# Where and in what shape one weight matrix is loaded in a decode layer: four DMAs early, or 65 spread over the run

## The chip, the cores and the metric

The kernel runs on one core of a Trainium2 chip. The metric is the device time of one execution in microseconds. Before the change it was 1316.74 us, the median of three runs (1316.66 to 1317.19). One more execution was taken by the hardware profiler; all rows shown come from it.

## The reference

One transformer layer decodes one token for each of 4 sequences: layer norm, attention of 32 heads over a cache of 8192 positions, output projection and residual, layer norm, gated feed-forward block, residual. All inputs are bfloat16.

```
B, Sq, D = 4, 1, 512;  H, Sk, Dh = 32, 8192, 128;  F = 1792

q = (layernorm(x) @ wq).reshape(B, Sq, H, Dh).transpose(0, 2, 1, 3)
scores = einsum("bhqd,bhkd->bhqk", q, k_cache) * Dh ** -0.5
p = softmax(scores)
o = einsum("bhqk,bhkd->bhqd", p, v_cache)
h = x + o.transpose(0, 2, 1, 3).reshape(B, Sq, H * Dh) @ wo
n = layernorm(h)
out = h + einsum("bsf,fd->bsd", sigmoid(n @ w_gate) * (n @ w_up), w_down)
```

The two caches hold 4 x 32 heads of 8192 x 128 values each: 128 heads of K and 128 of V, 2 MB apiece, 537 MB together. Each byte is used once. wq and wo have 4 MB each, the three feed-forward matrices 1.8 MB each.

## The kernel before

**Tiling.** A "head" below is one pair of sequence and head, numbered 0 to 127. K's or V's head is one slot of the tile KV, which has eight slots: 128 partitions, 16 KB on each (64 rows of the cache in a row). The PE engine transposes K in blocks of 128 x 128 (L360); ACT and DVE in turn copy the results out of PSUM (L370, L372); PE multiplies them with q (L385). Eight heads make a group, and the 16 groups go through the softmax one after the other. V's head is used nine heads later (LAGH = 9), as it lies in its slot (L469; L481 in the last group). When a group's 8 heads are done, the group's result is brought into the tile OT (L521), and `project` (L490 to L504) multiplies it with the two of wo's 32 head blocks that belong to this group (L498) and adds it to the residual. Group g needs the head blocks 2g and 2g + 1.

**Weights.** wq and wo use the same memory, the tile Wreg (128 partitions of 32 KB), one after the other: wo may be asked for only when the q projection (L533) has read wq. wo lies in HBM as 32 blocks of 128 rows of 512 values, so its view in Wreg takes from each partition's 32 KB one run of 1 KB for each head block.

**Loads and their order.** All DMAs are issued by the SP engine, in one queue and in the order of the list `order` (L305 to L315). Heads of K and V alternate from K's head 9 on (K 9, V 0, K 10, V 1, ...). Into this list are put wq behind K's head 0, wo's four pieces behind K's heads 2, 3, 4 and 5 (L312), w_gate before V's head 125, w_up and w_down at the end. A K or V is issued by `emit_head` (L271): it takes the next of the eight slots in rotation and waits until the job that held the slot has been read. `pump` (L324) takes from the list whatever can be put in the program at that point. A head is one DMA of 2 MB with one run of 16 KB per partition (L277); K's head 0 and V's head 127 come in four pieces (L274).

`emit_wo` (L300) issues one piece: one DMA of 1 MB, 128 partitions with eight runs of 1 KB each, and its token goes into the list t_wo. Each piece has a semaphore of its own (wo0 to wo3), and every DMA adds 16 to its semaphore when it has landed. `project` waits for all four tokens, `*t_wo` (L501).

**The end.** After V's head 127 come the last projection, the second layer norm, the gate and up products (L593), the down product in two halves (L609) and the output's DMA (L619).

Of the kernel before, what the change touches and what calls it, by code (L numbers as in the profile page):

```python
# [13 lines left out]
NKT = 16  # L14
LAGH = 9
GH = 8


class _Prog:
# [27 lines left out]
    def emit(self, eng, fn, waits=(), incs=1):  # L47

        todo = self._waits(eng, waits)
        tok = self.token(eng, incs) if incs else None  # L50

        def run(e):
            for key, v in todo:
                e.wait_ge(self.sems[key], v)
            made = fn(e)
            made = made if isinstance(made, list) else [made]
            if incs:
                assert len(made) == incs
                for m in made:
                    m.then_inc(self.sems[eng], 1)  # L60

        self.ops[eng].append(run)
        return tok
# [14 lines left out]
def bass_sequential_preLN__mha_block_cached__glu_gated_glu__decode_kernel(  # L78
# [20 lines left out]
    NH = B * H  # L99
    NG = NH // GH  # L100
    SCALE = float(DH) ** -0.5
# [3 lines left out]
    prog = _Prog()  # L105
    emit = prog.emit

    with ExitStack() as es:
        def SB(name, shape, dt):
            return es.enter_context(nc.sbuf_tensor(name, shape, dt))  # L110

        ident = SB("ident", [128, 128], BF16)
        identf = SB("identf", [128, 128], FP32)
        M8 = SB("M8", [128, GH], FP32)
        Gmat = SB("Gmat", [128, 128], FP32)
# [10 lines left out]
        q_all = SB("q_all", [128, NH], BF16)  # L126
        Lq = SB("Lq", [128, 2, GH * W], BF16)
        KV = SB("KV", [128, NSL, R * 128], BF16)
        kTc = SB("kTc", [128, NKT, 512], BF16)
        S_sb = SB("S_sb", [128, 512], FP32)  # L130
        E_sb = SB("E_sb", [128, 512], BF16)
        PT = SB("PT", [128, 2, NK * GH * 32], BF16)
        mpart = SB("mpart", [128, 1], FP32)
        mrow = SB("mrow", [1, GH], FP32)
        negmb = SB("negmb", [128, 1], FP32)
        sig = SB("sig", [128, 1], FP32)
        rsum = SB("rsum", [128, 1], FP32)
        O_sb = SB("O_sb", [128, 512], FP32)
        OT = SB("OT", [128, 2, GH], BF16)
        sg_sb = SB("sg_sb", [128, NFT * B], FP32)  # L140
# [7 lines left out]
        wo_v = Wreg[:, :].rearrange("p (h f) -> p h f", h=H)  # L148
# [39 lines left out]
        def cols(t, c):  # L188
            return t[:, c:c + NDC * (B - 1) + 1:NDC]
# [107 lines left out]
        t_wo = []  # L297
        t_qproj = []

        def emit_wo(i):  # L300
            src = A_wo.rearrange("(h p) f -> p h f", p=128)
            t_wo.append(prog.dma("sp", f"wo{i}", lambda e: e.dma_start(  # L302
                wo_v[:, 8 * i:8 * (i + 1), :], src[:, 8 * i:8 * (i + 1), :]), [t_qproj[0]]))

        order = []  # L305
        for n in range(NH):
# [2 lines left out]
        order.sort()  # L309
        order = [(k, n) for _, _, k, n in order]  # L310
        order.insert(1, ("wq", 0))
        for i, after in enumerate((2, 3, 4, 5)):  # L312
            order.insert(order.index(("k", after)) + 1, ("wo", i))
        order.insert(order.index(("v", NH - 3)), ("wg", 0))
        order += [("wu", 0), ("wd", 0)]  # L315
# [8 lines left out]
        def pump():  # L324
            while next_dma[0] < len(order) and ready(*order[next_dma[0]]):
                kind, n = order[next_dma[0]]
                next_dma[0] += 1
                if kind == "k":
                    emit_head("k", n, k_src(n), t_k, "k0p" if n == 0 else "")
                elif kind == "v":  # L330
                    emit_head("v", n, v_src(n), t_v, "vl" if n == NH - 1 else "")
                elif kind == "wq":
                    emit_wq()
                elif kind == "wo":
                    emit_wo(n)
                else:
                    emit_weight(kind)
# [152 lines left out]
        def project(g, t_ot):  # L490
            ob = g % 2

            def f(e):
                ins = None
                for c in range(NDC):
                    for hh in range(2):
                        h = 2 * g + hh
                        ins = e.matmul(cols(bank[XO][:, 64:64 + NDC * B], c), wo_v[:, h, 128 * c:128 * (c + 1)],  # L498
                                       OT[:, ob, B * hh:B * (hh + 1)], start=(hh == 0), stop=(hh == 1))
                return ins  # L500
            t = emit("pe", f, [t_ot, *t_wo])  # L501
            st_["ot"][ob] = t
            st_["h"] = st_["xo"] = emit("dve", lambda e: e.tensor_tensor(
                sth[:, 0:NDC * B], sth[:, 0:NDC * B], bank[XO][:, 64:64 + NDC * B], ALU.add), [t, st_["h"]])  # L504

        def finish(g):
            ob = g % 2
            t_oev[g] = emit("act", lambda e: e.activation(O_sb[:, :], bank[OBK], ACT.Copy),  # L508
                            [t_pvg[g], st_.get("sel")])
            box = {}  # L510

            def s1():
                def f(e):
                    ins = None
                    for q in range(4):
                        ins = e.matmul(bank[XO][:, 0:GH], O_sb[:, 128 * q:128 * (q + 1)],  # L516
                                       selq[:, q:q + 29:4], start=(q == 0), stop=(q == 3))
                    return ins
                t = emit("pe", f, [t_oev[g], t_sel, st_["xo"]])
                st_["sel"] = t  # L520
                box["ot"] = emit("dve", lambda e: e.tensor_copy(OT[:, ob, :], bank[XO][:, 0:GH]),  # L521
                                 [t, st_["ot"][ob]])

            def s2():
                project(g, box["ot"])
            return [(4, s1), (6, s2)]
# [22 lines left out]
        for u in range(4 * (NH + LAGH)):  # L549
# [20 lines left out]
            if vu >= 0:  # L570
                pv(vu // 4, vu % 4)
                if vu % 32 == 31 and vu // 32 < NG - 1:
# [8 lines left out]
        t_ot = emit("dve", lambda e: e.tensor_copy(OT[:, gl % 2, :], bank[OBK][:, 0:GH]),  # L581
                    [t_pvg[gl], st_["ot"][gl % 2]])
        project(gl, t_ot)
        t_hn, _ = layernorm(sth, st_["h"], 1, hnT, bank[XS], st_["xs"])

# [91 lines left out]
```

## Time and profile before

| What | Value |
|---|---|
| median of the runs | 1316.74 us |
| profiled execution, its own time | 1317.24 us |
| its span in the profile | 1315.5 us |
| HBM read | 550.77 MB, 419 GB/s over the span |
| K heads, 127 whole ones | 2048 KB each, 28.7 us from issue to landing (median) |
| V heads, 127 whole ones | 2048 KB each, 33.1 us |
| wo, 4 pieces | 1024 KB each, 14.1 us; issued at 21.4, 25.7, 32.1 and 41.5 us |
| wq, 4 pieces | 1024 KB each, 11.7 us |
| SP at L302 (wo's first piece), wait for the q projection | 15.0 us |
| first projection (L498) | 159.7 us |
| last projection (L498) | 1303.3 us |

The span is the time from the first to the last instruction that the profiler saw; the execution's own time is 1.74 us longer. The part 2 of the page cuts the span into 40 slices and gives the busy tenths of each engine; part 3 gives the DMA queues (q1 carries what the program asks for, q8 and q14 fetch instructions); part 4 follows the work that ended last back to the start and adds up its time by engine. "Issue to landing" is the time from SP's instruction to the last completion step of its DMA, with the time in the queue behind earlier DMAs in it.

### The profile page before, as it was taken

The page shows a single profiled execution, that of the slowest core. Times are in us where ns is not written, and L with a number is a line of the kernel's source. Part 1 is how long each engine was busy: PE and PEld are TensorE (multiplying, and loading weights), DVE is VectorE, ACT ScalarE, POOL GpSimd, SP SyncE. Part 2 cuts the span into 40 slices and gives each one's busy share as a digit, 9 for nine tenths or more (in the row PEclk, how much of TensorE's full clock was granted, in tenths as well). Part 3 has the DMA queues.
Part 4 walks back from the last instruction along what each step waited for, and adds up shares of the span by engine and source line. Part 5 has one row for each costly group of instructions (what it writes and reads, how often), then busy time and mean ns, then how long its engine had stood idle before and what let it go on. Part 6 is the DMA issues. An engine that isn't in the chain of part 4 may idle for free.

```text
span 1315.5 us, 29564 instructions
## 1 busy us (share of the span) xinstructions
PE 1016.4 (77%) x13385; PEld 671.9 (51%) x13385; DVE 721.1 (55%) x1210; ACT 608.7 (46%) x1095; POOL 9.0 (1%) x11
## 2 busy tenths in 40 slices
PE   6887877877788787887788778788887878778764
PEld 5654544545455454554455445455554545545443
DVE  5774655556555565555556456555555656556520
ACT  3664544545444454444445445454444545445420
POOL 2000000000000000000000000000000000000000
PEclk8988888888888888788888888888788888888865
DMA  9999999999999999999999999999999999999996
GB/s 381 415 427 426 427 427 427 425 428 425 428 425 426 427 425 428 424 427 426 427 426 426 426 428 424 427 425 428 427 424 426 426 428 425 426 427 428 425 411 245
DMA packets 45510, 552.68 MB, mean 420 GB/s; under 512 B 4420, under 2 KB 10312, under 8 KB 12360
## 3 DMA queue, kind: packets, MB, share of 16 engines
q1 hardware_dynamic: 45384, 550.79, 99.0%
q8 instruction: 105, 1.72, 0.5%
q14 instruction: 21, 0.17, 0.0%
HBM read 550.77 MB, written 0.00 MB: 419 GB/s over the span
## 4 chain that ended last, share of the span: by engine, by line
DMA 81%; PE 16%; SPq 2%; ACT 0%; issue 0%; DVE 0%
DMA KV<-in_A_v_cache_dram 76%; PE PS L360 10%; PE PS L385 3%; PE PS L469 3%; DMA KV<-in_B_w_down_dram 2%; DMA KV<-in_A_k_cache_dram 1%; SPq L277 1%; DMA Wreg<-in_A_wq_dram 1%; SPq L302 0%; SPq L295 0%; ACT kTc L370 0%; SPq L274 0%; ACT L422 0%; PE PS L533 0%; PE PS L481 0%
## 5 line engine op out<-in xcount | busy, mean ns | idle before, releaser
L372 DVE CAST kTc<-PS 128x512 bf16<-128x512 f32 x1024 | 676.1, 692 | 484.4 <-PE PS L360 481.6
L370 ACT ACTIVATE kTc<-PS 128x512 bf16<-128x512 f32 x1024 | 573.4, 595 | 648.2 <-PE PS L360 646.2
L360 PEld LDWEIGHTS PS<-ident,KV 128*128 128x128 bf16 x8192 | 547.5, 109 | 252.3 <-ACT kTc L370 135.7
L360 PE MATMUL PS<-ident,KV 128*128 128x128 bf16 x8192 | 654.7, 240 | 12.8 <-DMA KV<-in_A_k_cache_dram 10.4
L469 PE MATMUL PS<-KV,PT 128*32 128x512 bf16 x1920 | 216.8, 442 | 242.2 <-DMA KV<-in_A_v_cache_dram 242.2
L385 PE MATMUL PS<-kTc,Lq 128*32 128x512 bf16 x2048 | 227.1, 435 | 1.1 <-DVE Lq L545 0.6
L469 PEld LDWEIGHTS PS<-KV,PT 128*32 128x32 bf16 x1920 | 52.4, 99 | 273.9 <-DMA KV<-in_A_v_cache_dram 273.6
L385 PEld LDWEIGHTS PS<-kTc,Lq 128*32 128x32 bf16 x2048 | 53.5, 95 | 64.6 <-issue 19.1
L481 PE MATMUL PS<-PT,KV 128*128 128x1 bf16 x512 | 14.9, 165 | 18.0 <-DMA KV<-in_A_v_cache_dram 15.4
L481 PEld LDWEIGHTS PS<-PT,KV 128*128 128x128 bf16 x512 | 14.3, 104 | 18.6 <-DMA KV<-in_A_v_cache_dram 15.9
L516 PE MATMUL PS<-selq,O_sb 128*128 128x8 f32 x120 | 16.7, 266 | 7.1 <-ACT O_sb L508 7.1
L516 PEld LDWEIGHTS PS<-selq,O_sb 128*128 128x128 f32 x120 | 15.3, 200 | 10.0 <-ACT O_sb L508 10.0
L409 DVE TENSOR_REDUCE mrow<-PS 1x8 f32<-1x128 f32 x16 | 4.5, 279 | 29.2 <-PE PS L405 29.2
L205 ACT ACTIVATE lnw<-lnw 128x4 f32<-128x4 f32 x2 | 0.4, 205 | 38.9 <-DVE lnw L202 38.9
L581 DVE CAST OT<-PS 128x8 bf16<-128x8 f32 x1 | 0.2, 167 | 32.6 <-PE PS L481 32.6
L521 DVE CAST OT<-PS 128x8 bf16<-128x8 f32 x15 | 2.5, 167 | 19.5 <-PE PS L516 19.5
L422 ACT ACTIVATE E_sb<-S_sb,negmb 128x512 bf16<-128x512 f32 x16 | 11.6, 722 | 3.1 <-DVE negmb L420 2.6
L400 DVE TENSOR_REDUCE mpart<-S_sb 128x1 f32<-128x512 f32 x16 | 11.0, 686 | 3.1 <-ACT S_sb L398 1.5
L508 ACT ACTIVATE O_sb<-PS 128x512 f32<-128x512 f32 x15 | 9.0, 597 | 6.3 <-PE PS L469 6.3
L446 DVE CAST PT<-PS 128x512 bf16<-128x512 f32 x16 | 10.9, 682 | 0.7 <-PE PS L438 0.7
L398 ACT ACTIVATE S_sb<-PS 128x512 f32<-128x512 f32 x16 | 9.6, 597 | 1.2 <-PE PS L385 1.1
L405 PE MATMUL PS<-identf,mpart 128*1 128x128 f32 x32 | 7.5, 325 | 2.4 <-DVE mpart L400 2.4
(67 smaller groups left out, 119.5 us busy)
## 6 DMA issues: line engine op xcount, KB each, us to landing
KV<-in_A_k_cache_dram SPq DMA_DIRECT2D x127, 2048.0 KB, 28.7
KV<-in_A_v_cache_dram SPq DMA_DIRECT2D x127, 2048.0 KB, 33.1
Wreg<-in_A_wq_dram SPq DMA_DIRECT2D x4, 1024.0 KB, 11.7
Wreg<-in_A_wo_dram SPq DMA_DIRECT2D x4, 1024.0 KB, 14.1
KV<-in_A_k_cache_dram SPq DMA_DIRECT2D x4, 512.0 KB, 5.7
KV<-in_A_v_cache_dram SPq DMA_DIRECT2D x4, 512.0 KB, 26.6
KV<-in_B_w_gate_dram SPq DMA_DIRECT2D x1, 1792.0 KB, 28.1
KV<-in_B_w_up_dram SPq DMA_DIRECT2D x1, 1792.0 KB, 26.4
```

Of the source, the lines that this page charges most:

```text
L277: done[n] = [prog.dma("sp", f"sl{slot}", lambda e: e.dma_start(KV[:, slot, :], src), w)] * 4
L360: ins = e.matmul(bankT[g % NTB][:, 128 * i:128 * (i + 1)], KV[:, slot, r * 128:(r + 1) * 128], ident[:, :], start=True, stop=True)
L370: t_copy[g] = emit("act", lambda e: e.activation(kTc[:, ks, :], bankT[g % NTB][:, :], ACT.Copy), w)
L372: t_copy[g] = emit("dve", lambda e: e.tensor_copy(kTc[:, ks, :], bankT[g % NTB][:, :]), w)
L385: mms.append(e.matmul(PS[32 * j:32 * (j + 1), 512 * SBK:512 * (SBK + 1)], Lq[:, g % 2, off:off + 32], kTc[:, (n * NK + k) % NKT, :], start ...
L398: t_sev[g] = emit("act", lambda e: e.activation(S_sb[:, :], bank[SBK], ACT.Copy), [t_score[32 * g + 31], st_.get("exp")])
L400: t_mx = emit("dve", lambda e: e.tensor_reduce(mpart[:, :], S_sb[:, :], AX.X, ALU.max), [t_sev[g], st_.get("p1")])
L422: box["a2"] = emit("act", lambda e: e.activation(E_sb[:, :], S_sb[:, :], ACT.Exp, bias=negmb[:, 0:1], scale=SCALE, accum_out=sig[:, 0:1]), ...
L446: st_["xs"] = t_ptc[g] = emit("dve", lambda e: e.tensor_copy(dst, src), [t, t_pt0, t_pvg.get(g - 2)])
L469: mms.append(e.matmul(PS[32 * j:32 * (j + 1), 512 * OBK:512 * (OBK + 1)], PT[:, pb, o:o + 32], KV[:, slot, 512 * k:512 * (k + 1)], start=f ...
L481: ins = e.matmul(bank[OBK][:, i:i + 1], KV[:, slot, 128 * r:128 * (r + 1)], PT[:, pb, o:o + 1], start=(r == 0), stop=(r == R - 1))
L516: ins = e.matmul(bank[XO][:, 0:GH], O_sb[:, 128 * q:128 * (q + 1)], selq[:, q:q + 29:4], start=(q == 0), stop=(q == 3))
```

## The change

Three things are changed, all of them about wo.

The pieces stand elsewhere in the order: behind K's heads 9, 30, 62 and 94 in place of 2, 3, 4 and 5. They still wait for the q projection.

The pieces are cut otherwise. Pieces 0, 1 and 2 (eight head blocks each) and the first half of piece 3 (four) are loaded by 16 DMAs each, and each of these takes eight partitions that are 4 apart: 32a + j, 32a + j + 4, ..., 32a + j + 28 for a and j from 0 to 3. The second half of piece 3 is one DMA of 128 partitions. This makes 65 DMAs: 48 of 64 KB, 16 of 32 KB and one of 512 KB. All DMAs of a piece add to the piece's semaphore, and the token of the last stands for the piece.

A projection waits for the one piece that holds its head blocks, t_wo[g // 4], and no longer for all four.

```diff
+WO_PIECES = (((0, 8, 8),), ((8, 16, 8),), ((16, 24, 8),), ((24, 28, 8), (28, 32, 16)))
+WO_AFTER = (9, 30, 62, 94)
...
         def emit_wo(i):
+
             src = A_wo.rearrange("(h p) f -> p h f", p=128)
-            t_wo.append(prog.dma("sp", f"wo{i}", lambda e: e.dma_start(
-                wo_v[:, 8 * i:8 * (i + 1), :], src[:, 8 * i:8 * (i + 1), :]), [t_qproj[0]]))
+            for lo, hi, k in WO_PIECES[i]:
+                if k == 16:
+                    parts = [slice(0, 128)]
+                else:
+                    parts = [slice(32 * a + j, 32 * a + j + 29, 4) for a in range(4) for j in range(4)]
+                for ps in parts:
+                    t = prog.dma("sp", f"wo{i}", lambda e, ps=ps, lo=lo, hi=hi: e.dma_start(
+                        wo_v[ps, lo:hi, :], src[ps, lo:hi, :]), [t_qproj[0]])
+            t_wo.append(t)
...
-        for i, after in enumerate((2, 3, 4, 5)):
+        for i, after in enumerate(WO_AFTER):
             order.insert(order.index(("k", after)) + 1, ("wo", i))
...
-            t = emit("pe", f, [t_ot, *t_wo])
+            t = emit("pe", f, [t_ot, t_wo[g // 4]])
```

## The prediction

> **What bounds the kernel now.** I read the page first: the slices of part 2, the queues of part 3 and the chain of part 4.
>
> ```profile
> span 1315.5 us, 29564 instructions
> PE 1016.4 (77%) x13385; PEld 671.9 (51%) x13385; DVE 721.1 (55%) x1210; ACT 608.7 (46%) x1095; POOL 9.0 (1%) x11
> DMA  9999999999999999999999999999999999999996
> q1 hardware_dynamic: 45384, 550.79, 99.0%
> q8 instruction: 105, 1.72, 0.5%
> DMA 81%; PE 16%; SPq 2%; ACT 0%; issue 0%; DVE 0%
> ```
>
> No compute engine is above 77%, the sixteen DMA engines are busy in every slice but the last, and the chain is 81% DMA. The kernel is its 552 MB stream, so what matters is where the sixteen are *not* all busy. Stretches from the view by windows (last two columns: mean busy share of the sixteen, GB/s):
>
> ```profile
> 1100.00:1200.00 100.00, 82.62 (x1060) 54.10 (x1056) 59.19 (x102) 50.75 (x92) 0.00 (x0) 0.86 1.01 426
> 1280.00:1300.00 20.00, 6.32 (x218) 6.08 (x219) 0.00 (x0) 0.00 (x0) 0.00 (x0) 0.50 0.81 317
> 1300.00:1312.00 12.00, 6.61 (x198) 6.02 (x196) 1.84 (x11) 1.71 (x3) 0.00 (x0) 0.50 0.59 212
> ```
>
> Against 1.01, the last 32 us miss 20 x 0.20 + 12 x 0.42 = 9.0 us per engine. From 1292 to 1302 us the share is 0.53: about half the engines work and half are done. Why shows in the completion events. A K or V DMA makes sixteen completion steps, one per engine. For V's head 123 (issued at 1249.2 us) they come 0, 0.1, 0.3, 0.4, 0.8, 2.0, 5.9 and 9.5 us after the first, and then 18.6, 19.0 ... 20.2 us; for V's last whole head the eighth stands at 10.4 and the last at 20.8. Early on all sixteen lie within 1.2 us. Each of q8's 105 instruction fetches throws one engine back by 1.55 us (between two DMAs one of the sixteen steps moves from 9.09 to 10.66), in rotation over eight engines: 105 / 8 x 1.55 = 20.3 us, which is the lag. The other eight (I call them the leading ones) never carry q8, but one of them is thrown back 1.0 us at each of nine fetches on the small instruction queue (q14) and ends at 10.4. Which eight are which the trace does not say by number; where two packets of the two groups start in the same nanosecond, the leading one's record stands first in 23 of 25 cases, so the groups look like a lower and an upper half of one order.
>
> **What is removed and moved.** Before, each of four output-weight DMAs takes all sixteen engines for 2.67 us (first completions 28.05 to 30.71, 35.60 to 38.27, 43.17 to 45.88, 50.77 to 53.43 us): 64 rows of 1 KB per engine, 41.8 ns each, 10.7 us in all. Removing them from the first 60 us saves nothing by itself, since the bytes are asked for later. SP's wait for the q projection, 15.0 us at L302, goes: K's heads 3 to 7 are asked for at about 6 us. It is worth nothing, since the queue held work through it (share 1.03 in 10 to 20 us). The projections wait for one piece instead of four. The first runs at 159.7 us and every fourth after that needs a new piece, some 318 us apart (159.7, 477, 795, 1113); the pieces stand behind K's heads that landed at 75, 284, 602 and 920 us. So 80 to 190 us of slack covers them; the wait costs nothing, and were the cover gone it would be what a piece is late.
>
> **What is added: 64 DMAs of eight rows.** Pieces 0 to 2 are 16 DMAs each of 8 x 8 rows of 1 KB, piece 3 is 16 of 8 x 4 and one of the old form with 4 heads, 65 in place of 4. That a DMA of few rows takes few engines shows in x's load: four rows, four data packets, four completion steps. Eight rows then sit on at most eight engines, and by the order above I take the leading eight. For each of these: 3 x 128 + 64 rows x 41.8 ns = 18.7 us, 1.3 for the last four heads, 64 completion packets of 9 ns for 4, 0.5: 20.6 us against 10.7, **+9.9**. For the fetch eight: 1.3 against 10.7, **-9.4**. Then the last fetch engine ends at 20.8 - 9.4 = 11.4 of the old scale and the six undisturbed leading ones at 9.9 to 11.9: balanced. But the leading engine that already lagged ends at 10.4 + 9.9 = 20.3, against 20.8 before. Every K and V waits for all sixteen, so of 9 us possible **-0.5** remains.
>
> [...] The row of this trace is K's first head in four 512 KB pieces: first completions at 4.55, 5.84, 7.21, 8.47 us, 1.3 apart for 8 rows of 159 ns; fixed parts overlap, and I take none.
>
> **SP and the rings.** SP issues 61 more DMAs at 0.33 to 0.43 us, 20 to 26 us in all, beside 1114 us in which L277 waits: free. Not free is that the queue holds a limited number of rows. SP's own timeline:
>
> ```profile
> 21.42 0.38 SPq L302 DMA_DIRECT2D Wreg<-in_A_wo_dram  x1
> 21.84 3.83 SPq L277 DMA_DIRECT2D KV<-in_A_k_cache_dram  x1
> ...
> 34.66 6.82 SPq L277 DMA_DIRECT2D KV<-in_A_k_cache_dram  x1
> 41.53 0.44 SPq L302 DMA_DIRECT2D Wreg<-in_A_wo_dram  x1
> 42.01 9.40 SPq L277 DMA_DIRECT2D KV<-in_A_k_cache_dram  x4
> ```
>
> A K behind a piece of 65 descriptors per engine (64 rows, one step) held SP for 3.8 to 7.8 us, where 0.33 to 0.43 is usual; after 49.8 us, with the last old piece still queued, it took in more until 9 + 65 + 7 x 9 = 137 were outstanding per engine, so I put the limit near 140. A new piece is 16 x 9 = 144 on the leading engines, on top of some six K and V of 9 each. I expect SP to stick in the middle of a piece until the slowest leading engine has drained its K and V, some 30 us; the next K is queued behind. The fetch eight, with no rows of the piece, then run dry and start again together with the rest. Each piece so wipes out the lags, and the fetch engines' spared 9.4 us are spent idle. Two costs follow. After the last piece (near 925 us) the fetch engines lag anew: 29 fetches / 8 x 1.55 = 5.6 us against 3 x 1.0 for the slow leading one, less 0.3 of head start: **+2.3**. And at each restart the leading engine itself may wait. The bound below is nothing (SP issues in about the 0.34 us that eight rows of 41.8 ns take), above 4 x 2.2 = 8.8 us (an empty queue, as at the start: issue at 1.15, first completion at 4.6 us, less 1.25 of data). I take 0.35 each, **+1.4**, nearer the lower end since small DMAs stay queued while SP goes on.
>
> Where two engines write the same partitions no row tells: half of the small DMAs go to partitions 64 to 127, which the other eight also fill. The bounds are 0 and half speed for that half, 3.5 x 2.67 = 9.4 us; I take 0, since by the paragraph above the other eight are mostly idle then.
>
> **Sum.** -0.5 + 2.3 + 1.4 = +3.2 us. The profiled execution took 1317.24 us (span 1315.5 and 1.74 around it), so it would be 1320.4; the median of the runs is 0.5 lower, so **1319.9 us**. A change under 0.2% (2.6 us) I count as none.
>
> **Rivals.** *Balance:* the slow leading engine's delays are absorbed in the restarts or it gets fewer rows, and all engines end near 11.9 of the old scale: 20.8 - 11.9 = 8.9 us less, 1307.8 at best, 1312 if half of it comes. For it: the 9.0 idle us above, and that 9.4 fits a lag of 8 to 10 between the means of the halves. Against: the sixteen steps, where one leading engine stands at half the lag. *Nothing shifts to the end:* SP does not stick, or the rows spread over all engines; -0.5 to 0, 1316.2 to 1316.7. For it: six K and V were taken in within 3 us behind the fourth old piece. *Overload (slower):* the rows land on engines that carry q8, or meet the other eight's writes at full price. One fetch engine among the eight is enough: 20.8 + 9.9 = 30.7 against 20.8, +9.9, **1326.6**; it decides as soon as a q8 engine ends later than the slow leading one. For it: no row shows which engines eight rows take. Against: the order of equal stamps. [...]
>
> **Chances.** Forecast 0.42, of which 0.27 is above 2.6 us and 0.15 within; balance 0.20; nothing shifts 0.17; overload 0.21. So faster 0.20, same 0.32, slower 0.48. The forecast's own range is 1316.2 (no sticking) to 1327.3 (restarts at 8.8). As both signs hold much of the chance the range reaches to half of the balance and to the overload with a little over: 1311.5 to 1327.5.
>
> **What would show it.** In the changed profile, the eight-row DMAs make eight completion steps or sixteen. The last sixteen steps of V's head 123 within 6 us mean that the lags were wiped out; one step alone near 20, that nothing stuck; eight near 30, overload. A V or K behind a piece holds SP for tens of us, or not. The windows after 1280 us show whether the share stays near 1 to the end: if so, balance has come and my slow leading engine was wrong. If SP's small issues take far more than 0.43 us each without the ring being full, the free 61 DMAs were wrong.

## The result and the profile after

The changed kernel took 1329.08 us (median; 1328.34 to 1330.92) beside 1316.66 us of the kernel before on the same chip: 12.4 us more, ratio 1.0094, 95% interval 1.0083 to 1.0106. The forecast was 1319.9, its range ended at 1327.5. The span grew from 1315.5 to 1326.6 us.

The page of the kernel after: span, engine and DMA slices, queues, and the chain.

```profile
span 1326.6 us, 29627 instructions
DMA  9999999999999999998999999999999999999997
GB/s 384 398 411 425 426 427 427 426 370 425 427 426 427 426 426 427 428 422 366 426 426 427 426 428 425 427 427 395 426 426 426 428 428 425 427 427 427 425 424 277
q1 hardware_dynamic: 45848, 550.79, 98.4%
q8 instruction: 105, 1.72, 0.5%
DMA 76%; PE 19%; SPq 5%; issue 0%; ACT 0%; DVE 0%
```

The same bytes and the same 105 instruction fetches; a slice is 33.2 us, and the rate dips in the slices in which pieces 0 to 3 of wo are loaded (the second and third, the ninth, the nineteenth and the twenty-eighth). SP's share of the chain has grown from 2% to 5%. Its own timeline around piece 2 (start, duration, line, DMA):

```profile
573.81 0.33 SPq L279 DMA_DIRECT2D KV<-in_A_k_cache_dram  x1
574.18 29.89 SPq L311 DMA_DIRECT2D Wreg<-in_A_wo_dram  x16
604.12 0.44 SPq L279 DMA_DIRECT2D KV<-in_A_v_cache_dram  x1
```

SP sticks for 29.9 us in the lump of sixteen, as forecast; in the other lumps for 33.7, 31.4 and 27.6. What the DMA engines do at the end of that, by the view of windows (last two columns: mean busy share of the sixteen, GB/s):

```profile
592.00:596.00 4.00, 4.00 (x58) 2.43 (x55) 2.92 (x5) 2.43 (x5) 0.00 (x0) 0.87 1.01 426
596.00:600.00 4.00, 3.11 (x52) 2.03 (x49) 2.41 (x5) 2.01 (x5) 0.00 (x0) 1.00 0.81 326
600.00:604.00 4.00, 3.54 (x53) 2.12 (x52) 3.38 (x6) 2.67 (x6) 0.00 (x0) 1.00 0.46 154
604.00:608.00 4.00, 0.00 (x0) 0.00 (x0) 0.13 (x1) 0.00 (x0) 0.00 (x0) 0.84 0.75 254
608.00:612.00 4.00, 0.00 (x0) 0.00 (x0) 0.00 (x0) 0.00 (x0) 0.00 (x0) 0.50 1.01 430
...
1300.00:1312.00 12.00, 4.74 (x160) 4.50 (x160) 0.00 (x0) 0.00 (x0) 0.00 (x0) 0.50 0.94 373
1312.00:1323.00 11.00, 6.22 (x183) 5.71 (x184) 1.84 (x11) 1.71 (x3) 0.00 (x0) 0.50 0.54 181
```

The eight engines without rows run dry (0.46 of the sixteen at work in 600 to 604 us), and from 608 us on all are at work again (1.01). The eight-row DMAs make eight completion steps (4868 packets of 4 bytes on q1, where before had 4404), so eight engines share one. The lags are wiped out behind the first three pieces: the sixteen steps of the next V lie within 0.8, 1.3 and 1.1 us, behind the fourth within 4.5. All that had been forecast, in the main. At the end it differs: the sixteen steps of V's head 123 stand 10.7 us apart (20.2 before), where the forecast had them within 6, and two engines stand by themselves, at 10.1 and 10.7, with the other fourteen below 7.3.

The *last* completion of each K and V tells most. Against the same DMA of before, and averaged over the K and V between two pieces, it stands 10.6 us early ahead of the first piece (wo is still to come), then 5.1 early, 0.4 late, 6.0 late and 11.5 late behind the four pieces; a single K or V differs from these means by up to 1 us. Each piece stops the slowest engine for 5.5 us, about what 128 rows x 41.8 ns = 5.4 are. The forecast had the slowest engine spared those rows. So the question was which engine is the slowest, and whether rows are all that it pays.

### The profile page after: what moved, and what is told of

Its sections match the earlier page's. It is cut to its first block, busy times and chain, and to the rows that moved or that the text cites. A ratio compares the mean times of both kernels' runs of the same rounds, so it can differ in the third digit from the quotient of the medians.

```text
span 1326.6 us, 29627 instructions
## 1 busy us (share of the span) xinstructions
PE 1016.6 (77%) x13385; PEld 670.1 (51%) x13385; DVE 720.4 (54%) x1210; ACT 607.8 (46%) x1095; POOL 9.0 (1%) x11
## 4 chain that ended last, share of the span: by engine, by line
DMA 76%; PE 19%; SPq 5%; issue 0%; ACT 0%; DVE 0%
DMA KV<-in_A_v_cache_dram 73%; PE PS L370 11%; SPq L311 4%; PE PS L395 4%; PE PS L479 3%; DMA KV<-in_A_k_cache_dram 2%; DMA KV<-in_B_w_down_dram 1%; SPq L297 0%; SPq L279 0%; PE PS L415 0%; SPq L276 0%; PE PS L427 0%; PE PS L491 0%; PE PS L448 0%; ACT kTc L380 0%
## 5 line engine op out<-in xcount | busy, mean ns | idle before, releaser
L395 PEld LDWEIGHTS PS<-kTc,Lq 128*32 128x32 bf16 x2048 | 53.5, 95 | 64.6 <-issue 19.4
L432 ACT ACTIVATE E_sb<-S_sb,negmb 128x512 bf16<-128x512 f32 x16 | 11.5, 722 | 3.1 <-DVE negmb L430 2.9
```

The costliest lines, as they stand in the source:

```text
L395: mms.append(e.matmul(PS[32 * j:32 * (j + 1), 512 * SBK:512 * (SBK + 1)], Lq[:, g % 2, off:off + 32], kTc[:, (n * NK + k) % NKT, :], start ...
L432: box["a2"] = emit("act", lambda e: e.activation(E_sb[:, :], S_sb[:, :], ACT.Exp, bias=negmb[:, 0:1], scale=SCALE, accum_out=sig[:, 0:1]), ...
```

## The experiments

Most experiments use one edit: wo is loaded by a list of units (a K head to stand behind, piece, partitions, head blocks) in place of the loop over pieces. Each is then told by its list.

```diff
-        def emit_wo(i):
+        def emit_wo(unit):
+            i, ps, lo, hi = unit
...
+            t_wo[i] = prog.dma("sp", f"wo{i}", lambda e: e.dma_start(
+                wo_v[ps, lo:hi, :], src[ps, lo:hi, :]), [t_qproj[0]])
...
-        for i, after in enumerate(WO_AFTER):
-            order.insert(order.index(("k", after)) + 1, ("wo", i))
+        for after, unit in reversed(WO_UNITS):
+            order.insert(order.index(("k", after)) + 1, ("wo", unit))
```

**First: places or shape?** Two kernels hold one half of the change each: e1_place the old DMAs of 128 partitions at the new places with a wait for each piece, e2_shape the 65 DMAs at the old places.

```diff
+ALL = slice(0, 128)
+EIGHT = [slice(32 * a + j, 32 * a + j + 29, 4) for a in range(4) for j in range(4)]
+# e1_place
+WO_UNITS = [(after, (i, ALL, 8 * i, 8 * i + 8)) for i, after in enumerate((9, 30, 62, 94))]
+# e2_shape
+WO_UNITS = [(after, (i, ps, 8 * i, 8 * i + (4 if i == 3 else 8))) for i, after in enumerate((2, 3, 4, 5)) for ps in EIGHT]
+WO_UNITS += [(5, (3, ALL, 28, 32))]
```

> The changed places and waits, with the old shape: four DMAs of 128 partitions. Empty queue (SP, held in a lump of 16 small DMAs, asks for no K or V for 30 us, and all sixteen engines then stand still for about 5.5 us a lump): nothing of this can happen, 1316.7 us within 1. If the places themselves cost something: above 1319. Overload (the eight engines simply have 20.6 us of work on wo where they had 10.7): 1316.7 too.

> The changed shape at the old places, behind K's heads 2 to 5. Empty queue: the lumps cost the same four stops, 1327 to 1330, and the lags of the sixteen completion steps are near 18 us at the end, as before, since the lumps lie at the start. Overload or shared partitions: the engines with rows stand some 10 us later at the end than before against the others, and the time is near 1316.5 (slow leading engine) or 1326 (fetch engines loaded).

e1 took 1316.59 us (ratio 0.9998, 0.9988 to 1.0008): places and waits cost nothing. e2 took 1336.36 (1.0148, 1.0133 to 1.0163): the shape is the cost, and at the old places it is dearer than forecast. SP's timeline of e2 shows why:

```profile
21.46 11.61 SPq L307 DMA_DIRECT2D Wreg<-in_A_wo_dram  x16
33.12 0.44 SPq L281 DMA_DIRECT2D KV<-in_A_k_cache_dram  x1
33.60 11.51 SPq L307 DMA_DIRECT2D Wreg<-in_A_wo_dram  x16
45.15 0.53 SPq L281 DMA_DIRECT2D KV<-in_A_k_cache_dram  x1
```

Sixteen issues take 11.5 us, 0.72 each, with one K between two lumps. The K land at 40.8, 53.2 and 65.1 us, 12.2 apart, where a K and a piece of the old form take 4.9 + 2.67 = 7.6: 4.6 us a piece, 18.5 in all of the 19.4 lost. With nothing queued, SP's issue is the pace. In the change some 30 us of K and V are queued ahead of each lump and cover it.

**Second: an empty queue?** My first theory for the change was the restart behind each lump. e3_spread puts the same 65 DMAs one behind each K, so nothing runs dry; e4_half does so with half of the head blocks and loads the rest in the old form.

```diff
+# e3_spread
+WO_UNITS = [(2 + n // 2, (0, ps, 0, 8)) for n, ps in enumerate(EIGHT)]
+WO_UNITS += [(last - 15 + n, (i, ps, 8 * i, 8 * i + (4 if i == 3 else 8)))
+             for i, last in ((1, 30), (2, 62), (3, 94)) for n, ps in enumerate(EIGHT)]
+WO_UNITS += [(94, (3, ALL, 28, 32))]
+# e4_half: blocks 8 * i to 8 * i + 4 so, and
+WO_UNITS += [(last, (i, ALL, 8 * i + 4, 8 * i + 8)) for i, last in enumerate((9, 30, 62, 94))]
```

> The same 65 DMAs, but one behind each K head (two for the first piece, behind K's heads 2 to 9) in place of a lump of 16. Empty queue: SP is never held for long, K and V stay queued, and the loss is gone: 1316.2 by the slow leading engine (20.3 us of lag against 20.8 before), and up to 1318 if 0.7 us of SP each matters. Overload of fetch engines: 1326. Two engines writing the same partitions at half speed: up to 1326.

> Spread as in the run before, but only half of each piece (4 of 8 head blocks) goes by eight-row DMAs, the rest by one DMA of 128 partitions. If the leading eight get the rows and nothing else costs: leading engines 16.3 us of wo against 10.7, so the slow one ends at 10.4 + 5.6 = 16.0; fetch engines 5.35 against 10.7, so their last ends at 20.8 - 5.35 = 15.5; both 4.8 us before 20.8: 1311.9 us, faster than both kernels. Overload of fetch engines: 1322. Shared partitions at full price: about 1317.

Both missed: e3 took 1339.43 (1.0175, 1.0160 to 1.0190), e4 1329.40 (1.0095, 1.0080 to 1.0110). Without any lump it is worse than the change, so the restart is not the main cost. The page of e3:

```profile
span 1339.7 us, 29627 instructions
GB/s 381 380 406 427 427 426 410 403 408 426 427 427 427 426 424 422 406 400 419 420 427 427 427 426 426 418 415 404 427 426 428 426 426 426 427 424 415 427 414 176
```

The rate falls to 400 to 410 in stretches where the share of busy engines stays at 1.01: the engines are at work but slower. The 32617 packets of 16 KB (32512 carry K and V, 105 are instruction fetches) last 1259.1 us per engine before and 1275.4 in e3. And they are slowed in only half of the stretch of each piece. Piece 1's sixteen DMAs run from 131 to 294 us, and the windows of its two halves differ:

```profile
135.00:205.00 70.00, 55.07 (x702) 35.62 (x700) 39.38 (x66) 33.31 (x60) 0.00 (x0) 0.87 1.01 426
212.00:294.00 82.00, 63.91 (x760) 41.25 (x761) 42.28 (x70) 35.76 (x65) 0.00 (x0) 0.81 1.01 403
```

In the 10 us around each of the first eight DMAs the 16 KB packets lose 0.4 to 1.5 us of engine time in all against their usual 0.61 us each, around each of the last eight 9.5 to 10.5. The first eight go to partitions 0 to 63, the last eight to 64 to 127.

**Third: which partitions?** First with everything loaded: e5_low takes the rows of partitions 0 to 63 in eight-row DMAs and those of 64 to 127 in one DMA of 64 partitions a piece, e6_high the other way round; e7_lowlump is e5 in lumps.

```diff
+# e5_low (e6_high: a in (2, 3) and slice(0, 64))
+EIGHT = [slice(32 * a + j, 32 * a + j + 29, 4) for a in (0, 1) for j in range(4)]
+REST = slice(64, 128)
+WO_UNITS = [(last - 7 + min(n, 7), (i, ps, 8 * i, 8 * i + 8))
+            for i, last in enumerate((9, 30, 62, 94)) for n, ps in enumerate(EIGHT + [REST])]
+# e7_lowlump: as e5_low, with (last, ...)
```

> The output weights' rows of partitions 0 to 63 come in eight-row DMAs (8 a piece, 32 in all, one behind each of the eight K up to heads 9, 30, 62 and 94), the rows of partitions 64 to 127 in one DMA of 64 rows x 8 heads a piece. If that DMA is dealt to all sixteen engines, the leading eight carry 384 rows of 1 KB and the others 128, where before each had 256: 128 x 41.8 ns = 5.3 us are moved. In the two spread runs K's and V's 16 KB packets were slowed only in the stretches in which eight-row DMAs went to partitions 64 to 127 (about 10 us of engine time for each such DMA, some 0.5 for each to partitions 0 to 63). Theory (the upper partitions are the cost, since the other eight engines write there): no packet is slowed beyond the short 64-row DMAs, the slow leading engine ends at 10.4 + 5.3 = 15.7 and the last of the others at 20.8 - 5.3 = 15.5 against 20.8 before: 5.1 us faster, 1311.6 us, at most 1314 if the four 64-row DMAs cost 0.5 each. Rival (each row in an eight-row DMA costs some 50 ns more wherever it goes, as the half-spread run has it with as many rows): about 1329. Rival (61 or 33 more issues, not the rows): about 1323.

> The mirror image: the rows of partitions 64 to 127 in eight-row DMAs, those of 0 to 63 in one DMA of 64 rows x 8 heads a piece; the same count of DMAs, the same bytes, the same rows per engine. Theory (upper partitions): all 2048 rows of eight-row DMAs meet the other engines' writes. The full spread lost 22.7 us for 1792 such rows, the half spread 12.7 for 1024: 12.4 to 12.7 ns of the end per row, so 25 to 26 us lost, 1342 us, and K's and V's 16 KB packets take 17 to 18 us more per engine than before (the full spread: 16.3). Rival (every row costs the same): about 1329, like its mirror image. Rival (issues): the same as its mirror image.

> The same DMAs as in the run with the lower partitions spread, but each piece's nine in one lump behind K's heads 9, 30, 62 and 94, as the change has its sixteen. A piece is 8 x 9 + 33 = 105 descriptors for a leading engine where the change had 144. If only the upper partitions cost, and the queue does not run dry: 1311.6 to 1314. If SP still sticks in each lump and the other eight run dry, what is moved is lost: the last engine stops for the leading engines' 96 rows, 4.0 us a piece, against 2.7 before, 4 x 1.3 = 5.3 less what the wiped-out lags give, with some 2 us for each restart: 1317 to 1326.

e5 1340.81 (1.0170, 1.0156 to 1.0184), e6 1357.23 (1.0302, 1.0288 to 1.0316), e7 1330.81 (1.0105, 1.0091 to 1.0119). The absolute numbers of e5 and e6 missed, since I had not seen what the 64-partition DMA does. The page of e5:

```profile
GB/s 381 394 394 428 425 427 426 427 374 425 426 428 427 427 425 427 426 402 371 427 427 427 426 425 428 426 425 357 415 426 425 428 426 426 426 427 427 424 414 211
```

The dips are where the four 64-partition DMAs run (394, 374, 371, 357), and there are none around the eight-row ones. A 64-partition DMA makes sixteen completion steps, so sixteen engines write half of the partitions, and around piece 2 the mean 1 KB row takes 80 to 110 ns in place of 46. Of e7's 13.7 us over before, 5.3 are moved rows (128 x 41.8 ns on each of eight engines); the rest is put down to the same DMAs, whose rows take up to 89 ns around piece 2, but no run parts it. The pair still says something: 16.4 us between e5 and its mirror image. The next four kernels drop the 64-partition DMA, that is, they leave half of wo out: f1_low loads partitions 0 to 63 alone, spread; f2_high 64 to 127 alone; f3_next 0 to 63 by eight neighbours; f4_lowlump is f1 in lumps.

```diff
+# f1_low (f2_high: a in (2, 3); f3_next: slice(8 * m, 8 * m + 8) for m in range(8))
+EIGHT = [slice(32 * a + j, 32 * a + j + 29, 4) for a in (0, 1) for j in range(4)]
+WO_UNITS = [(last - 7 + n, (i, ps, 8 * i, 8 * i + 8))
+            for i, last in enumerate((9, 30, 62, 94)) for n, ps in enumerate(EIGHT)]
+# f4_lowlump: as f1_low, with (last, ...)
```

> The output weights' rows of partitions 0 to 63 in eight-row DMAs, 8 a piece, one behind each of the eight K up to heads 9, 30, 62 and 94; the rows of partitions 64 to 127 are left out, 2 MB less. The leading eight carry the 256 rows each that they had before, the other eight none (256 x 41.8 ns = 10.7 us less). Theory (what costs is an engine that writes partitions which another engine is filling; here the leading eight write only partitions that they fill themselves): no 16 KB packet is slowed; the slow leading engine ends at 10.4, the last of the others at 20.8 - 10.7 = 10.1, so 10.4 us less than before: 1306 us. Rival (each row of an eight-row DMA costs some 50 ns more, wherever it goes): 256 x 50 ns = 12.8 on the leading eight, which end at 23: 1319.

> The mirror image: the rows of partitions 64 to 127 in eight-row DMAs, those of 0 to 63 left out. Same count, bytes, rows per engine and places as its twin. Theory: 2048 rows meet the other eight's writes; at the 12.4 to 12.7 ns of the end per such row of the two spread runs that is 25 us over the twin, at the difference of the two runs with a 64-row DMA 16: 1322 to 1332 us, with slowed 16 KB packets in the four stretches. Rival (the partitions don't matter): the same as the twin.

> As the run with the lower partitions alone, but each eight-row DMA takes eight neighbouring partitions instead of eight that stand 4 apart. Theory A (it is only the halves that count, partitions 0 to 63 against 64 to 127): the same as the twin, 1306. [...]

> As the run with the lower partitions alone, but each piece's eight DMAs in one lump behind K's heads 9, 30, 62 and 94. A lump is 72 descriptors for a leading engine, beside six K or V of 9 each 126, under the 140 or so at which SP sticks in the change's lumps of 144. Theory: no long stick, no packet slowed, the same as the spread twin within 2 us. Rival (a lump costs by itself, in SP's 0.70 us an issue and the restart): 2.4 us a lump, as much as the change lost over the forecast's 1.4 in all: some 10 us over the twin.

| kernel | us | ratio, interval | 16 KB packets, us per engine |
|---|---|---|---|
| before | 1316.97 | | 1259.1 |
| f1_low | 1316.06 | 0.9994, 0.9984 to 1.0003 | 1259.3 |
| f2_high | 1331.93 | 1.0113, 1.0098 to 1.0128 | 1277.1 |
| f3_next | 1334.81 | 1.0137, 1.0121 to 1.0152 | 1274.7 |
| f4_lowlump | 1316.73 | 0.9996, 0.9987 to 1.0006 | 1261.0 |

The page of f1, then that of f2:

```profile
span 1315.2 us, 29594 instructions
GB/s 381 425 426 427 426 427 427 425 428 426 425 427 427 426 426 426 427 425 428 427 427 423 426 427 427 426 421 428 426 426 425 427 425 421 429 426 428 425 407 195
```

```profile
span 1330.4 us, 29594 instructions
GB/s 376 384 420 425 427 425 405 404 412 426 426 427 428 425 427 422 404 404 420 423 428 425 427 427 426 414 404 404 421 425 427 426 424 426 425 429 425 425 416 216
```

f1 has a flat 421 to 429 up to its last slices, f2 has four holes (384, then 404 three times): the same DMAs, 64 partitions higher, slow the stream and cost 15.9 us. I call this the **clash**, and my reading of it is two engines on the same partitions; no trace names the engine that fills a partition, so the reading is not shown. It is 2048 rows, 256 on each of eight engines: 15.9 / 256 = 62 ns of the end for each row of an engine, on top of the row's own 41.8. f3 shows that the halves are not the rule, since eight neighbours clash in the lower half too: 1334.8 us against f1's 1316.1, with 16 KB packets of 1274.7 us per engine against 1259.3.

Two things about SP show in these runs. The time of f4 is as expected, but "no long stick" was not: SP sticks in its lumps for 23 to 26 us. Around piece 2 its eight issues take 0.71, 0.68, 0.68, 0.68, 2.24, 2.83, 10.53 and 4.24 us, so it sticks at the fifth, with at most 10 x 9 = 90 descriptors ahead for an engine (six K and V, four eight-row DMAs), where the prediction put the limit near 140. And the price of an issue is not that of eight rows: eight neighbouring partitions (f3) cost SP half of what eight partitions 4 apart do (f1). The line of f1, then that of f3:

```profile
509.46 0.71 SPq L306 DMA_DIRECT2D Wreg<-in_A_wo_dram  x1
508.58 0.35 SPq L306 DMA_DIRECT2D Wreg<-in_A_wo_dram  x1
```

f1 itself had been expected at 1306 and took 1316.1: no packet is slowed, yet the 10 us do not come. The completion steps show where. For K and V around three points of f1, the sixteen steps in us after the first (each row: issue time, then the steps):

```
 496.8  0.0 0.4 4.9 5.0 5.7 6.2 7.6 7.9 8.0 8.1 8.6 9.4 9.9 10.0 13.0 13.8
 497.9  0.0 0.4 5.3 5.3 6.0 6.5 7.9 7.9 8.0 8.2 8.6 9.7 9.9 10.0 13.3 14.1
...
1127.6  0.0 0.0 0.1 0.1 0.8 2.0 5.4 7.1 7.2 7.3 7.8 9.0 9.2 9.3 17.4 18.2
1139.2  0.0 0.0 0.1 0.1 0.8 2.0 5.5 7.1 7.2 7.8 8.9 9.0 9.2 9.3 17.4 19.8
1158.5  0.0 0.0 0.1 0.1 0.7 2.0 5.5 7.1 7.2 7.8 8.9 9.0 9.2 9.3 19.0 19.8
```

Between the first two rows one eight-row DMA ran, and eight steps moved by 0.33 (8 x 41.8 ns): the last two among them (13.0, 13.8). In the last three rows the last two each move by 1.6, the jump of an instruction fetch. So **two of the eight engines that take the rows carry q8**, and two of the others never do. My two groups were wrong by a pair.

**Fourth: is it those two?** I assumed that a DMA of four, six or seven rows goes to the first four, six or seven of the eight engines. The rest of wo is left out.

```diff
+# g4_rows, g6_rows, g7_rows: N = 4, 6, 7
+FEW = [slice(32 * a + j, 32 * a + j + 4 * N - 3, 4) for a in (0, 1) for j in range(4)]
+WO_UNITS = [(last - 7 + n, (i, ps, 8 * i, 8 * i + 8))
+            for i, last in enumerate((9, 30, 62, 94)) for n, ps in enumerate(FEW)]
```

> As the run with the lower partitions alone, spread, but each DMA takes the first four of its eight rows; the other rows are left out. If four rows go to the first four of the eight engines, these carry the 256 rows each that they had before and the other twelve none. In the run with eight rows two of the eight stood 17 to 21 us behind at the end, with q8's jumps of 1.55 us among their steps, and six that carried no rows stood at 7 to 10.6 with the same jumps. Theory (two of the engines that eight rows take carry q8, so the forecast's two groups were wrong): if neither of the two is among the first four, the last engine ends at some 10 instead of 20.8 and the time is 1306 us; if one is, 1316.5. Rival (small DMAs hold two of the eight engines up by themselves, whichever): two of the four stand at 20 again, 1316.5, whatever the number of rows, here and with six and seven.

> The same with the first six of the eight rows, so the first six engines. Theory: 1306 if both engines with q8 are the last two, 1316.5 if one of them is among the six; never faster than the run with four rows. The number of engines 17 us or more behind at the end is the number of q8's engines among the six. Rival: 1316.5.

> The same with the first seven rows. Theory: one engine stands at 17 or more and the time is 1316.5 if the two are the seventh and eighth; otherwise as many as are among the seven. Rival: 1316.5 with two of them behind.

g4 took 1306.50 us (0.9920, 0.9905 to 0.9935), g6 1315.86 (0.9992, 0.9983 to 1.0002), g7 1316.53 (0.9996, 0.9987 to 1.0005). The steps of one K or V of each near 1238 us:

```
g4  0.0 0.1 0.2 1.2 10.4 10.5 15.8 17.9 18.0 18.5 18.5 19.9 19.9 20.4 20.4 20.6
g6  0.0 0.0 0.2 2.1  2.3  3.5  8.0  9.5  9.9  9.9 10.3 11.1 11.2 11.4 11.6 20.0
g7  0.0 0.1 0.7 1.5  1.9  3.2  8.6  9.7  9.8 10.0 11.0 11.2 11.2 11.6 20.0 20.8
```

With four rows no engine stands apart (I take the zero of that list for an engine with neither rows nor q8, which would end 256 x 41.8 ns = 10.7 us earlier than with rows). With six rows one engine stands 8 us behind the rest, with seven two. The DMAs of the three runs make four, six and seven completion steps. So, if they go to the first four, six and seven engines of the eight, one engine with q8 is the fifth or sixth, the other the seventh. The tail of g4 by windows:

```profile
1280.00:1300.00 20.00, 10.94 (x342) 10.19 (x342) 1.84 (x11) 1.71 (x3) 0.00 (x0) 0.50 0.76 290
1300.00:1312.00 12.00, 1.18 (x29) 0.91 (x29) 0.45 (x2) 0.00 (x0) 0.00 (x0) 0.72 0.02 4
```

After 1300 us it has almost nothing left to load, where the kernel before had a share of 0.59. g4 is no faster version of the kernel, since it loads a quarter of wo; it shows that its 256 rows on each of four engines cost the end nothing. The count of late engines, 0, 1, 2 and 2 for four, six, seven and eight rows, agrees with a fixed order; no trace gives the engines by number.

**Fifth: how the change's 12.4 us divide.** h2_ownlump is the change, lumps and all, with the rows for partitions 64 to 127 written 64 partitions lower, over blocks that are loaded again or have been used, so that as in f1 nothing should clash; what belongs in the upper half is left out but for the last four blocks. h3_ownspread is h2 with e3's places. h1_highlump has the clash without added rows: partitions 64 to 127 alone (the lower half is left out), in lumps.

```diff
+# h2_ownlump, h3_ownspread
+            if ps.start >= 64:
+                own = slice(ps.start - 64, ps.stop - 64, 4)
+                to = (lo + 8) % H
+                t_wo[i] = prog.dma("sp", f"wo{i}", lambda e: e.dma_start(
+                    wo_v[own, to:to + hi - lo, :], src[ps, lo:hi, :]), [t_qproj[0], t_wo.get(i - 1), t_proj.get(3)])
+                return
+# h1_highlump: f2_high with (last, ...)
```

> The rows of partitions 64 to 127 alone, in lumps of eight DMAs behind K's heads 9, 30, 62 and 94; the rows of 0 to 63 are left out. Each of the eight engines has the 256 rows it had before, the two among them that carry q8 too, so without any clash of two engines on one partition the time is that of before, 1316.5. Its spread twin took 1331.9, so 15.9 were the clash there. The change lost 12.4 us, of which 9.9 are the 237 added rows on q8's engines (the overload rival's sum); if the other 2.5 are the clash at the ends of its lumps, this run shows them: 1319. Rival (a lump protects nothing): 1332.

> The change's own 65 DMAs in its own lumps, with its bytes and sources, but those for partitions 64 to 127 are written to partitions 64 lower (over rows that are loaded again or no longer needed), so no engine writes partitions that another fills; the rows of 64 to 127 are left out but for the last four heads. Theory: the two engines that carry q8 and rows end at 20.8 + 9.9 = 30.7 against 20.8: 1316.7 + 9.9 = 1326.6, and what the change took beyond that, 2.5, was the clash. Rival (the 2.5 are SP's sticking and the restarts): 1329.1 as the change.

> The same, with the DMAs one behind each K as in the full spread run, which took 1339.4. Theory: 1326.6 again, with no slowed packet; so of the full spread's 22.7 us 9.9 are the rows on q8's engines and 12.8 the clash. Rival (spreading costs by itself): above 1330.

h2 took 1326.52 us (1.0079, 1.0065 to 1.0093), h3 1325.29 (1.0062, 1.0049 to 1.0076): 9.4 and 8.1 over before, near the 9.9 of the rows on q8's engines, in lumps or spread, with 16 KB packets of 1260.4 and 1260.1 us per engine. (The 9.9 are 224 more rows on each of them, 9.4, and 60 more completion packets, 0.5; the 237 in the expectation is 9.9 divided by 41.8 ns.) So e3, which differs from h3 by the clash, loses 1339.4 - 1325.3 = 14.1 us to it: 63 ns for each of the 224 rows of an engine that go to partitions 64 to 127. The windows of h2 around piece 2 look like the change's:

```profile
596.00:600.00 4.00, 3.18 (x52) 2.14 (x52) 1.93 (x4) 1.95 (x4) 0.00 (x0) 1.00 0.84 339
600.00:604.00 4.00, 3.19 (x52) 2.02 (x44) 3.22 (x6) 2.39 (x5) 0.00 (x0) 1.00 0.42 132
604.00:608.00 4.00, 0.00 (x0) 0.00 (x0) 0.00 (x0) 0.00 (x0) 0.00 (x0) 0.67 0.85 289
```

More than half of the engines stand idle for 4 us and it costs nothing, for they are not the late ones. h1 missed: 1333.29 (1.0122, 1.0108 to 1.0136), not 1319. A lump of these rows clashes as much as the same rows spread, although SP stuck 23 to 27 us in each. So the lump is not what spares the change, and the last run turns the order within it:

```diff
-                    parts = [slice(32 * a + j, 32 * a + j + 29, 4) for a in range(4) for j in range(4)]
+                    parts = [slice(32 * a + j, 32 * a + j + 29, 4) for a in (2, 3, 0, 1) for j in range(4)]
```

> The change itself with one edit: in each lump the eight DMAs to partitions 64 to 127 go first and those to 0 to 63 after them. The same DMAs, bytes, rows per engine and lumps, so the rows on q8's engines cost 9.9 us as in the change. The change took 1329.1, 2.5 more than that, although its rows for 64 to 127 meet the other engines' partitions; the lump of these rows alone took 1333.3, 16.1 over before. Theory (in the change the rows for 0 to 63 go first, by the time of the others the engines that fill 64 to 127 have run dry, and so little clashes): with the order turned the rows meet K and V at work: up to 1316.7 + 9.9 + 16.1 = 1343, at least 1334. Rival (SP's sticking for the 144 descriptors protects, whatever the order): 1329.

j1_highfirst took 1334.43 us (1.0130, 1.0113 to 1.0147), 5.4 more than the change by order alone (4.9 when each is taken against its own before), at the low end of what was expected. Its windows:

```profile
596.00:600.00 4.00, 1.86 (x28) 1.03 (x27) 2.14 (x4) 1.51 (x3) 0.00 (x0) 1.00 0.96 289
600.00:604.00 4.00, 2.63 (x24) 1.87 (x28) 0.84 (x2) 1.18 (x2) 0.00 (x0) 0.53 0.76 177
604.00:608.00 4.00, 4.00 (x44) 2.43 (x37) 1.93 (x4) 1.45 (x4) 0.00 (x0) 0.61 0.36 115
608.00:612.00 4.00, 2.27 (x36) 1.34 (x32) 2.56 (x4) 1.94 (x4) 0.00 (x0) 1.00 0.60 165
```

The first line has a share of 0.96 at 289 GB/s: the engines are busy, at seven tenths of the rate that goes with that share (0.96 / 1.01 x 427 = 406). In the change the rows for 0 to 63 go first, and by the time of the others the eight engines without rows have mostly run dry: around piece 2 no 16 KB packet starts between 601 and 605 us. Around the change's piece 3 they had not, being 6.6 us behind: there, from 922 to 924 us, a 16 KB packet lasts 1.0 to 1.1 us instead of 0.61, and the piece stops the last engine for 5.5 us, where its 96 rows are 4.0 (64 in eight-row DMAs, 32 in the old form). In h2, where the 16 KB packets are not slowed, the same means of the last completion move by 5.2, 5.2, 5.2 and 3.7 us with the four pieces, in the change by 5.5 each time: the clash costs the change some 0.3 us in each of the first three pieces and 1.8 in the fourth.

## Why the prediction was wrong

- **Where the rows land** is the step that failed: "by the order above I take the leading eight". Two of the eight carry q8. The term "-0.5" should have been +9.9, the overload's sum, which the prediction named and gave 0.21; h2 shows it as 9.4, h3 as 8.1. The evidence for the grouping, equal start stamps in 23 of 25 cases, fits a grouping that is right for six of eight engines. The price of the rows themselves (41.8 ns) was right.
- **Shared partitions, put at 0,** is the second step, and it carries the time past the range, which ended above the overload's 1326.6. What the change took beyond 1316.7 + 9.9 = 1326.6 is 2.5 us; against h2 it is 12.4 - 9.4 = 3.0, with intervals that overlap. j1 and f2 show the clash apart from it. The bound of 9.4 holds for the change but was too low as a bound: I took half speed, 41.8 ns a row, where f2 pays 62, and e3 loses 14.1 to these rows. The reason given, that the other eight are idle by then, holds for three of the pieces, and only because of the order.
- **Restarts (+1.4) and the lag after the last piece (+2.3)** are both near zero. h2 has sticking, idle engines and restarts, and ends no later than its rows make it. The late engines are among those that carry the rows, so the lags of the others, kept or wiped out, don't set the end. These two terms made the forecast "slower": that the sign came out is luck.
- **SP's 61 issues** were free in the change, as forecast, though their price was wrong: 0.68 to 0.72 us, not 0.33 to 0.43, because the partitions are 4 apart (f3 pays 0.35). At the old places they would have set the pace (e2).
- **SP sticking for some 30 us** came true, but not for the reason given: the limit near 140 descriptors does not carry over to eight-row DMAs, since f4 sticks with at most 90 ahead. What the limit counts stays open.
- **Right:** eight completion steps for a DMA, the lags wiped out (not wholly behind the last piece), places and waits worth nothing (e1). *Balance* fell with the grouping. *Nothing shifts* fell too, since SP stuck and the rows sat on eight engines.

Not tried: any version that takes bytes off the engines with q8 without a clash. The eight-row DMAs slowed K and V in f2 and f3 (16 KB packets of 1277.1 and 1274.7 us per engine against 1259.1), so I found nothing that beats the kernel before. That no such version exists is argued, not shown. Which of the fifth and sixth engine carries q8, if the rows do go to the first ones, is open as well.

## What to carry to other kernels

A DMA of few rows was a way of choosing engines here (four rows made four completion steps in g4, eight rows eight), and the choice has to be measured first: load a few rows with 4, 6, 7 and 8 of them, leave the rest out, and see which engines end late. Measure the partitions too: the same eight-row DMAs cost the end nothing for partitions 0 to 63 (f1) and 62 ns a row of an engine more for 64 to 127 (f2). And where the slowest engine bound the stream, the idle time of the others, however wide in the windows, was no cost: h2 stood at a share of 0.42 for 4 us, and its 9.4 us over before are what the added rows take.

## What the runs showed of the hardware

- Eight of the sixteen completion steps of a K or V fall behind under instruction fetches (V's head 123 before: eight steps at 18.6 to 20.2 us, the others within 9.5; 105 fetches / 8 x 1.55 us = 20.3). Of the eight engines that an eight-row DMA uses, two are among these (late engines: none with four rows, one with six, two with seven and eight; g4 1306.5 us, g6 1315.9, g7 1316.5, f1 1316.1).
- Eight-row DMAs to partitions 64 to 127 slow K and V: 256 rows of 1 KB on each of eight engines cost 15.9 us of the end (f2 against f1), and in the fourth lump of the change, from 922 to 924 us, a 16 KB packet lasts 1.0 to 1.1 us instead of 0.61. Eight partitions 4 apart in the lower half slow nothing (f1, 1316.1 us); eight neighbours do (f3, 18.7 us over f1), and around a DMA of 64 partitions with sixteen completion steps the rows take 80 to 110 ns in place of 46 (e5). That two engines on the same partitions are the cause is my reading.
- An eight-row DMA that the queue takes at once costs SP 0.68 to 0.72 us when its partitions are 4 apart, with 32 rows of 1 KB (e4) as with 64 (f1), and 0.34 to 0.35 us when they are neighbours (f3). SP sticks in a lump of eight of them (23 to 27 us, f4 and h1) when six K and V are queued.
